# Attention, MoE and gated MoE on one core: the attention's engines each a step apart

## The chip, the cores and the metric

One core of a Trainium2 chip runs one program. The metric is the device time of one execution in microseconds: 684.07 us is the median of three runs of the kernel before (683.9 to 685.65). Five engines work in queues of their own, each in the order in which its instructions were written: TensorE (PE, matrix products and transposes, results to PSUM), VectorE (DVE), ScalarE (ACT), GpSimd (POOL, which here works on SBUF only) and SyncE (SP, which starts the transfers). PSUM has eight banks, here of 512 numbers in each of 128 partitions.

## The reference

Causal attention over 2 batches, 12 heads, 448 positions and head size 64; its result, 896 tokens of 768 numbers, goes through a first MoE layer (one expert) and a second, gated one.

```python
scores = scale * q @ k.T;  scores = where(mask, -1e9, scores)
attn = exp(scores - max(scores));  attn = attn / (sum(attn) + 1e-9)
x = (attn @ v)                                   # to (896, 768)
h = x @ w_in;  g = where(h >= 1, h, where(h <= -1, 0, (h + 1)**2 / 4));  x = g @ w_out
xn = x / sqrt(mean(x*x) + 1e-6) * rms_g
out = (silu(xn @ w_gate) * (xn @ w_val)) @ w_out2
```

## The kernel before

**Products in pairs.** The weights arrive as 64-bit numbers. A *weight step* is a quarter of the work on one block of 128 x 768: scaling of a half on GpSimd (L146), the sign (L151), the high bits (L157) and the low bits (L163) on VectorE, and then the split into a rounded part and a rest on GpSimd (L172, L178). Each block of a layer is then multiplied in three products (L344, 128x448 each), rounded by rounded, rounded by rest, rest by rounded.

**Attention in units.** Two heads are done at a time, in halves of the partitions; such a pair is a *group*, six groups to a batch, twelve in all. A group has three *units*, n = 3g, 3g+1, 3g+2, by rows of the score matrix cut in blocks of 112: the last block row (448 columns for each head), the third and the first (336 and 112), the second (224). For a unit:
- `scores(n)`: on TensorE, for each of the two heads a product of an identity with the mask (L249) that opens the score bank, and the products of q and k (L254). Units take two of four banks in turn (0 to 3), so `scores(n)` waits until the exponentials of unit n-2 have read these banks;
- `maxima(n, j)`: VectorE's negative row maxima of head j (L260);
- `exps(n, j)`: ScalarE's exponentials with their sums (L268), to SBUF;
- `transposes(n)`: on TensorE, the blocks of the exponentials turned over (L284), into banks of a second ring, two for the first two units and one for the third;
- `evac(n, i)`: the copy of the i-th of these banks to SBUF, on ScalarE (L301) or VectorE (L303).

For a group there are besides: `factor` (reciprocals of the sums on VectorE, L309 and L310, and their broadcast on GpSimd, L311), `spread` (that broadcast turned over on TensorE, L317, and copied by ScalarE, L318), `pv` (the P·V products into bank 7, L329), `xsplit` (P·V times the reciprocals on VectorE, L335, and the two parts of X on GpSimd, L336 and L337), the scaling of q two groups ahead (`scale_q`, L228) and the loads.

**The second ring** has banks 4, 5 and 6, and one of them also serves `spread`. In the second batch bank 6 leaves it: columns 0 to 7 of the first MoE layer (first half of the tokens, whose X is then ready) are filled in between, in *parts* of three products (`push_in`, `pump`), six parts to a column, all in bank 6. When a column's six parts are done, `moe_act` works on it (ScalarE L352 and L353, VectorE L354), and only then may the next column begin in the bank. `fillin` takes as many parts as an even share of its calls asks for; what is left is done behind the loop by `pump(len(fill))`.

**What sets the order.** The order of each queue is written out by hand: the loop over n calls these functions, and each engine does its part in the order of the calls. `w_pace` calls weight steps, 0.15 blocks per turn of the loop in the first batch and 0.55 in the second, up to 13 blocks. Turn n of the loop before: scores of n+2; at the head of a group spread and P·V of the group before; transposes of n; then in turn maxima and exponentials of head 0 of n+1, the first copy of n, maxima and exponentials of head 1 of n+1, the second copy of n.

**Behind the attention** the MoE layers run as one dense stream of products on TensorE, with the weight steps beside it.

## Time and profile before

| | |
|---|---|
| median of three runs | 684.07 us |
| profiled execution, its time | 680.13 us |
| its span | 678.4 us |
| mean granted TensorE clock | 0.964 |
| PE / DVE / ACT / POOL busy | 625.6 / 417.5 / 226.1 / 259.9 us |
| DMA, mean | 96 GB/s, 65.03 MB |

The durations are those of one profiled execution; times in it count from the start of its span. A busy time is a mean over stages with different limits: the attention fills about the first 198 us, where TensorE has gaps, and the MoE layers the rest, where it has nearly none. A row that ends in "[1.11 <-ACT af L268]" says that the engine had been idle 1.11 us before it and that the end of ScalarE's line 268 released it. PEclk is the granted clock as a share of 2.4 GHz; at 0.5 it is 1.2 GHz.

### The profile page before, as it was taken

The numbers are of one execution on the slowest core, as the hardware profiler recorded it, in microseconds if no ns is written. First come the engines' busy times: TensorE is split into PE (matmuls) and PEld (weight loads), VectorE is DVE, ScalarE is ACT, GpSimd is POOL, SyncE is SP. The second block draws the span as 40 slices with busy tenths as digits, with TensorE's granted clock in tenths as the row PEclk, the third lists the DMA queues.
The fourth block names the chain that finished last, engine by engine and source line by source line (L and its number), as shares of the span: only waits on it lengthen the run. The fifth ranks groups of instructions, "written<-read, shape, count | busy, mean of one in ns | idle before, by whom it ended". The sixth has DMA issues, their size and how long they took to land.

```text
span 678.4 us, 8418 instructions
## 1 busy us (share of the span) xinstructions
PE 625.6 (92%) x3244; PEld 536.2 (79%) x3244; DVE 417.5 (62%) x547; ACT 226.1 (33%) x492; POOL 259.9 (38%) x207
## 2 busy tenths in 40 slices
PE   6777768977799999999999989999999999999997
PEld 3444435655589999989989978999999999999997
DVE  3435554644548577785153687998988877798300
ACT  3454444544434444422152225112122221332100
POOL 2332475644564645462000152244443344336200
PEclk9788989977899999999999998999999999999999
DMA  6123142313122444342000141223233243336101
GB/s 228 49 90 119 42 135 87 134 61 107 48 94 95 145 137 151 128 146 84 1 0 1 47 140 47 93 94 130 103 112 122 93 127 107 93 121 187 68 29 41
DMA packets 16696, 65.03 MB, mean 96 GB/s; under 512 B 2000, under 2 KB 6608, under 8 KB 16656
## 3 DMA queue, kind: packets, MB, share of 16 engines
q1 hardware_dynamic: 16656, 64.50, 28.9%
q8 instruction: 25, 0.41, 0.3%
q14 instruction: 15, 0.12, 0.1%
HBM read 61.74 MB, written 2.75 MB: 95 GB/s over the span
## 4 chain that ended last, share of the span: by engine, by line
PE 83%; DVE 7%; ACT 7%; issue 2%; DMA 0%; ACTq 0%; SPq 0%
PE b L344 42%; PE b L543 14%; PE b L653 13%; PE b L329 5%; PE b L254 4%; ACT af L268 4%; PE b L284 2%; DVE af L157 2%; DVE af L163 1%; ACT af L301 1%; DVE ar L498 1%; PE b L317 1%; PE b L249 1%; DVE nm L260 1%; DVE af L354 1%
## 5 line engine op out<-in xcount | busy, mean ns | idle before, releaser
L344 PE MATMUL b<-ar 128*128 128x448 f32 x1440 | 303.8, 370 | 11.8 <-DVE af L354 11.8
L344 PEld LDWEIGHTS b<-ar 128*128 128x128 f32 x1440 | 270.1, 189 | 39.6 <-DVE af L354 13.8
L178 POOL TENSOR_TENSOR ar<-af,ar 128x768 fp32r<-128x768 f32 x68 | 128.9, 1896 | 193.4 <-ACT ar L170 192.3
L543 PE MATMUL b<-ar 128*128 128x448 f32 x576 | 121.2, 371 | 3.8 <-DVE ar L498 3.4
L543 PEld LDWEIGHTS b<-ar 128*128 128x128 f32 x576 | 109.0, 190 | 15.6 <-DVE ar L498 4.6
L146 POOL TENSOR_SCALAR af<-af 128x768 f32<-128x768 f32 x68 | 73.2, 1077 | 93.4 <-DMA af<-in_w_out 44.4
L170 ACT CAST ar<-af 128x768 fp32r<-128x768 f32 x55 | 45.9, 835 | 174.0 <-DVE af L163 168.8
L163 DVE SCALAR_TENSOR_TENSOR af<-af 128x768 int32<-128x768 int32 x68 | 87.7, 1290 | 1.8
L653 PE MATMUL b<-ar 128*128 128x448 f32 x432 | 87.7, 365 | 0.0
L653 PEld LDWEIGHTS b<-ar 128*128 128x128 f32 x432 | 81.1, 188 | 6.4
L157 DVE SCALAR_TENSOR_TENSOR af<-af 128x768 int32<-128x768 int32 x68 | 78.4, 1153 | 1.8
L151 DVE TENSOR_SCALAR af<-af 128x768 int32<-128x768 int32 x68 | 53.5, 787 | 8.4 <-POOL af L146 8.4
L268 ACT ACTIVATE af<-b,nm 112x336 f32<-112x336 f32 (+2 forms) x96 | 47.4, 499 | 31.5 <-DVE nm L260 31.3
L498 DVE TENSOR_TENSOR ar<-af,ar 128x448 fp32r<-128x448 f32 x32 | 28.5, 893 | 47.7 <-ACT ar L497 47.5
L354 DVE SCALAR_TENSOR_TENSOR af<-af,b 128x448 f32<-128x448 f32 x32 | 19.8, 619 | 40.9 <-ACT af L353 40.8
L249 PE MATMUL b<-maskb,identb 112*112 112x112 bf16 (+1 forms) x72 | 16.0, 238 | 31.1 <-ACT af L268 29.0
L254 PEld LDWEIGHTS b<-af 64*112 64x112 f32 x192 | 16.0, 193 | 36.0 <-issue 27.3
L301 ACT COPY af<-b 112x448 f32<-112x448 f32 x48 | 25.6, 533 | 45.4 <-PE b L284 44.9
L619 DVE TENSOR_TENSOR af<-af 128x448 f32<-128x448 f32 x24 | 35.4, 1476 | 7.3 <-ACT af L617 6.3
L254 PE MATMUL b<-af 64*112 64x448 f32 (+3 forms) x192 | 37.0, 488 | 2.5 <-DVE af L228 2.5
L260 DVE TENSOR_REDUCE nm<-b 112x1 f32<-112x336 f32 (+2 forms) x96 | 36.8, 436 | 3.1 <-PE b L254 3.1
L497 ACT CAST ar<-af 128x448 fp32r<-128x448 f32 x32 | 18.0, 565 | 56.6 <-PE b L543 56.5
(52 smaller groups left out, 408.8 us busy)
## 6 DMA issues: line engine op xcount, KB each, us to landing
af<-in_w_out SPq DMA_DIRECT2D x28, 768.0 KB, 4.3
af<-in_w_in SPq DMA_DIRECT2D x16, 768.0 KB, 4.3
af<-in_w_gate SPq DMA_DIRECT2D x12, 768.0 KB, 4.2
af<-in_w_val SPq DMA_DIRECT2D x12, 768.0 KB, 4.3
af<-in_kT SPq DMA_DIRECT2D x12, 224.0 KB, 3.5
af<-in_qT SPq DMA_DIRECT2D x12, 224.0 KB, 3.8
af<-in_v SPq DMA_DIRECT2D x12, 224.0 KB, 2.7
out_T<-af SPq DMA_DIRECT2D x12, 224.0 KB, 2.0
```

Of the source, the lines that this page charges most:

```text
L146: nc.gpsimd.tensor_scalar(out=c, in0=c, scalar1=2.0 ** -112, scalar2=1.0, op0=ALU.mult, op1=ALU.mult)
L151: nc.vector.tensor_scalar(out=wt[n % 2].bitcast(I32), in0=words(n, 1, I32), scalar1=-2 ** 31, scalar2=0, op0=ALU.bitwise_and, op1=ALU.bitw ...
L157: nc.vector.scalar_tensor_tensor(out=t, in0=words(n, 1, I32), scalar=3, in1=t, op0=ALU.logical_shift_left, op1=ALU.bitwise_or)
L163: nc.vector.scalar_tensor_tensor(out=t, in0=words(n, 0, I32), scalar=29, in1=t, op0=ALU.logical_shift_right, op1=ALU.bitwise_or)
L170: nc.scalar.copy(dst[:, 0, :], wt[n % 2])
L178: nc.gpsimd.tensor_tensor(out=dst[:, 1, :], in0=wt[n % 2], in1=b32(dst[:, 0, :]), op=ALU.subtract)
L254: nc.tensor.matmul(bs[j][:C, o:o + (c + 1) * C], lhsT=q[r, c * C:(c + 1) * C], rhs=k[r, :(c + 1) * C], start=False, stop=True, skip_group_ ...
L260: nc.vector.tensor_reduce(out=stat[g][0][:C, j, c:c + 1], in_=sbank[n][j][:C, o:o + (c + 1) * C], axis=AX.X, op=ALU.max, negate=True)
L268: nc.scalar.activation(Pn[:C, j, poff[c]:poff[c] + w], sbank[n][j][:C, o:o + w], ACTF.Exp, bias=nm[:C, j, c:c + 1], accum_out=sums[:C, j, ...
L344: nc.tensor.matmul(out, lhsT=w[:, a, k * P:(k + 1) * P], rhs=x[:, c, k], start=(k == 0 and n == 0), stop=(k == NK - 1 and n == 2))
L543: nc.tensor.matmul(ybs[dm][:, :S], lhsT=w[:, a, dm * P:(dm + 1) * P], rhs=t[:, c], start=(n == 0 and i == 0), stop=(n == NM - 1 and i == 2))
L653: nc.tensor.matmul(ob[:, :S], lhsT=w2[dm][:, kk // NK, a, kk % NK], rhs=x[:, c], start=(kk == 0 and i == 0), stop=(kk == NF - 1 and i == 2))
```

## The change

The functions stay as they are; the loop calls them in another order; ahead of it only the scores of unit 0 are done. Turn n now has the scores of n+1, maxima and exponentials of n with the copies of n-2 among them, and the transposes of n-1 at its end; spread and P·V stand in the group's second turn, the X split in its third, `factor` in its first. The loop has one turn more. The filling-in starts with turn 24 (before 21) and counts on three calls of `fillin` per turn.

```diff
@@ -434,48 +434,47 @@
             quota -= k
 
     scores(0)
-    maxima(0, 0)
-    exps(0, 0)
-    maxima(0, 1)
-    exps(0, 1)
-    scores(1)
-    last = NN + 2
+    last = NN + 3
     for n in range(last):
         g, u = divmod(n, NU)
-        if n == NP * NU + 3:
+        if n == NP * NU + 6:
             for m in range(NFILL):
                 push_in(m, 0)
             tring.remove(6)
-            left[0] = 2 * (last - n)
-        if n + 2 < NN:
-            scores(n + 2)
-        if u == 0 and g:
-            spread()
-            pv(g - 1)
-            load_v(g + 1)
+            left[0] = 3 * (last - n)
+        if n + 1 < NN:
+            scores(n + 1)
         fillin()
+        side = nc.vector if g < NP else nc.scalar
+        old = 2 <= n < NN + 2
         if n < NN:
-            transposes(n)
-        more = n + 1 < NN
-        if more:
-            maxima(n + 1, 0)
-            exps(n + 1, 0)
+            maxima(n, 0)
+        if old and u == 1:
+            evac(n - 2, 0, nc.scalar)
         if n < NN:
-            evac(n, 0, nc.scalar)
-        if more:
-            maxima(n + 1, 1)
-            exps(n + 1, 1)
-        if n < NN and u < 2:
-            evac(n, 1, nc.vector if g < NP else nc.scalar)
-        if (n + 1) % NU == NU - 1 and more:
-            factor((n + 1) // NU)
+            exps(n, 0)
+        if old and u != 1:
+            evac(n - 2, 0, nc.scalar)
+            evac(n - 2, 1, side)
+        if n < NN:
+            maxima(n, 1)
+            exps(n, 1)
         if u == 0:
             if g:
+                factor(g - 1)
+        elif u == 1:
+            load_qk(g + 3)
+            if g:
+                spread()
+                pv(g - 1)
+                load_v(g + 1)
+                fillin()
+        else:
+            if g:
                 xsplit(g - 1)
-        elif u == 1:
             scale_q(g + 2, nc.gpsimd)
-        else:
-            load_qk(g + 3)
+        if 1 <= n <= NN:
+            transposes(n - 1)
         flush()
         w_pace(RATE[0] if n < NP * NU else RATE[1])
         fillin()
```

ScalarE, third group of the first batch (b_ numbers are PSUM tiles: b_273, b_274 and b_295, b_296 the scores of its second and third unit, b_319 and b_352 transposes of its first and second). Before:

```order
L268 ACTIVATE af,sums<-b_245,nm 112x448
L318 COPY af<-b_301 128x448
L268 ACTIVATE af,sums<-b_273,nm 112x336
L268 ACTIVATE af,sums<-b_273,nm 112x112
L301 COPY af<-b_319 112x4x112
L268 ACTIVATE af,sums<-b_274,nm 112x336
L268 ACTIVATE af,sums<-b_274,nm 112x112
L268 ACTIVATE af,sums<-b_295,nm 112x224
L301 COPY af<-b_352 112x4x112
L268 ACTIVATE af,sums<-b_296,nm 112x224
```

and now (scores b_271, b_272 and b_296, b_297; transposes b_289 of the unit before the group, b_331 of its first):

```order
L301 COPY af<-b_289 112x2x2x112
L268 ACTIVATE af,sums<-b_271,nm 112x336
L268 ACTIVATE af,sums<-b_271,nm 112x112
L268 ACTIVATE af,sums<-b_272,nm 112x336
L268 ACTIVATE af,sums<-b_272,nm 112x112
L318 COPY af<-b_313 128x448
L268 ACTIVATE af,sums<-b_296,nm 112x224
L301 COPY af<-b_331 112x4x112
L268 ACTIVATE af,sums<-b_297,nm 112x224
```

The copy of the first unit's transposes stood between the exponentials of the second unit; now it stands between those of the third.

GpSimd, X split (L336, L337), broadcast of the reciprocals (L311), scaling of q (L228) and weight steps, fourth group. Before:

```order
L336 TENSOR_SCALAR ar<-af 128x448
L337 TENSOR_TENSOR ar<-af,ar 128x448
L311 TENSOR_SCALAR af<-rs 112x512
L228 TENSOR_SCALAR af<-af 128x448
L172 TENSOR_SCALAR ar<-af 128x768
L178 TENSOR_TENSOR ar<-af,ar 128x768
```

and now:

```order
L336 TENSOR_SCALAR ar<-af 128x448
L337 TENSOR_TENSOR ar<-af,ar 128x448
L228 TENSOR_SCALAR af<-af 128x448
L311 TENSOR_SCALAR af<-rs 112x512
L146 TENSOR_SCALAR af<-af 128x768
L336 TENSOR_SCALAR ar<-af 128x448
```

The scaling of q has moved from behind the broadcast to in front of it.

TensorE, the end of the attention (L344 filled-in parts of columns, L284 transposes, L317 and L329 spread and P·V of the last group, then the dense products). Before:

```order
L284 MATMUL b_1415<-ident,af 112x112 x4
L344 MATMUL b_1407<-ar 128x448 x9
L284 MATMUL b_1447<-ident,af 112x112 x4
L344 MATMUL b_1407<-ar 128x448 x3
L317 MATMUL b_1462<-ident,af 128x112 x4
L329 MATMUL b_1468<-af 64x336 x2
L329 MATMUL b_1468<-af 64x112 x2
L329 MATMUL b_1468<-af 64x336 x2
L329 MATMUL b_1468<-af 64x224 x2
L329 MATMUL b_1468<-af 64x112 x2
L344 MATMUL b_1479<-ar 128x448 x18
L344 MATMUL b_1508<-ar 128x448 x18
```

and now:

```order
L284 MATMUL b_1416<-ident,af 112x112 x4
L344 MATMUL b_1406<-ar 128x448 x6
L317 MATMUL b_1432<-ident,af 128x112 x4
L329 MATMUL b_1438<-af 64x336 x2
L329 MATMUL b_1438<-af 64x112 x2
L329 MATMUL b_1438<-af 64x336 x2
L329 MATMUL b_1438<-af 64x224 x2
L329 MATMUL b_1438<-af 64x112 x2
L344 MATMUL b_1406<-ar 128x448 x9
L344 MATMUL b_1464<-ar 128x448 x18
L344 MATMUL b_1486<-ar 128x448 x18
L344 MATMUL b_1508<-ar 128x448 x18
```

Behind the last P·V there stood one column of 18 products and then the second half's columns; now half a column and two columns stand there first.

## Rows read from the trace of the kernel before

**Rows 1.** Stretches: us, busy (count) PE, PEld, DVE, ACT, POOL, clock, DMA, GB/s.
```profile
20.83:84.30 63.47, 47.92 (x332) 29.35 (x331) 30.50 (x72) 30.74 (x100) 24.37 (x26) 0.90 0.25 80
84.30:118.66 34.36, 25.21 (x157) 16.47 (x156) 18.54 (x30) 15.20 (x46) 21.24 (x18) 0.87 0.34 110
118.66:191.84 73.18, 60.51 (x346) 43.68 (x344) 39.27 (x67) 32.49 (x95) 38.83 (x34) 0.86 0.25 83
191.84:198.50 6.66, 5.88 (x40) 4.75 (x40) 4.24 (x4) 1.36 (x3) 5.49 (x5) 1.00 0.45 149
198.50:678.40 479.90, 472.49 (x2309) 434.10 (x2307) 317.19 (x356) 138.01 (x225) 164.72 (x111) 0.99 0.29 94
```

**Rows 2.** Page's costliest groups: busy, mean ns, idle before and its releaser.
```profile
L249 PE MATMUL b<-maskb,identb 112*112 112x112 bf16 (+1 forms) x72 | 16.0, 238 | 31.1 <-ACT af L268 29.0
...
L301 ACT COPY af<-b 112x448 f32<-112x448 f32 x48 | 25.6, 533 | 45.4 <-PE b L284 44.9
```

**Rows 3.** Timeline, third group: start us, us, engine, line, what.
```profile
34.05 2.11 PE L329 MATMUL b<-af 112*64 112x336 f32 x20
...
36.10 0.98 PE L284 MATMUL b<-ident,af 112*112 112x112 f32 x8
...
36.78 0.53 ACT L301 COPY af<-b 112x448 f32<-112x448 f32 x1 [1.17 <-PE b L284]
...
37.11 0.62 DVE L303 COPY af<-b 112x448 f32<-112x448 f32 x1 [3.86 <-PE b L249]
...
38.24 0.21 PE L249 MATMUL b<-maskb,identb 112*112 112x112 bf16 x1 [1.11 <-ACT af L268]
...
38.35 0.56 POOL L336 TENSOR_SCALAR ar<-af 128x448 fp32r<-128x448 f32 x1 [5.87 <-DVE af L335]
...
38.38 1.01 PE L254 MATMUL b<-af 64*112 64x448 f32 x4
...
41.34 1.10 DVE L260 TENSOR_REDUCE nm<-b 112x1 f32<-112x448 f32 x2
...
42.00 0.64 ACT L268 ACTIVATE af<-b,nm 112x448 f32<-112x448 f32 x1 [1.02 <-DVE nm L260]
```

**Rows 4.** Busy time in the group of rows 3.
```profile
34.05:45.30 11.25, 8.41 (x67) 5.33 (x66) 5.79 (x14) 6.21 (x20) 6.60 (x7) 1.00 0.33 117
```

**Rows 5.** Groups by shape, GpSimd, 20.9 to 84.4 us.
```profile
L337 POOL TENSOR_TENSOR ar<-af,ar 128x448 fp32r<-128x448 f32 x5 | 5.7, 1138 | 0.4
L311 POOL TENSOR_SCALAR af<-rs 112x512 f32<-112x512 f32 x5 | 4.4, 889 | 4.1 <-DVE rs L310 4.1
L228 POOL TENSOR_SCALAR af<-af 128x448 f32<-128x448 f32 x5 | 3.8, 761 | 0.0
L336 POOL TENSOR_SCALAR ar<-af 128x448 fp32r<-128x448 f32 x5 | 3.7, 741 | 33.9 <-DVE af L335 33.9
```

**Rows 6.** Groups by shape, VectorE, same stretch.
```profile
L157 DVE SCALAR_TENSOR_TENSOR af<-af 128x768 int32<-128x768 int32 x3 | 2.8, 921 | 0.0
```

**Rows 7.** Timeline, the dense products behind the last P·V.
```profile
194.73 9.59 PE L344 MATMUL b<-ar 128*128 128x448 f32 x46 [0.78 <-DVE af L354]
```

**Rows 8.** Timeline, border between two weight columns.
```profile
112.14 0.86 PE L344 MATMUL b<-ar 128*128 128x448 f32 x3
...
114.99 0.87 PE L344 MATMUL b<-ar 128*128 128x448 f32 x3 [1.99 <-DVE af L354]
```

**Rows 9.** Timeline, GpSimd's first X operation beside a weight step.
```profile
88.10 0.95 DVE L163 SCALAR_TENSOR_TENSOR af<-af 128x768 int32<-128x768 int32 x1
88.27 1.20 POOL L336 TENSOR_SCALAR ar<-af 128x448 fp32r<-128x448 f32 x1 [7.21 <-DVE af L335]
```

**Rows 10.** Timeline, TensorE at a lower granted clock.
```profile
58.87 3.80 PE L329 MATMUL b<-af 112*64 112x336 f32 x20
...
142.08 1.84 PE L254 MATMUL b<-af 64*112 64x448 f32 x4
...
146.25 1.70 PE L284 MATMUL b<-ident,af 112*112 112x112 f32 x8
```

## The prediction

> **What bounds the kernel now.** I read the page's costliest groups first, then the busy time by stretch, then one attention group instruction by instruction. Three things are to be seen.
>
> First, where the loss lies. From the first P·V product (20.83 us) to the twelfth (191.84) TensorE is busy 47.92 of 63.47 us, 25.21 of 34.36 and 60.51 of 73.18, at a mean granted clock of 0.86 to 0.90; behind it, 472.49 of 479.90 at 0.99 [rows 1]. So only the attention has idle time to give, 15.6 + 9.2 + 12.7 = 37.4 us, and a shift of the attention's end is carried to the end of the kernel nearly whole.
>
> Second, who waits. The largest waits there are ScalarE's copies of transposed blocks on TensorE's transposes (44.9 us of the page's 45.4), and TensorE's mask products on ScalarE's exponentials (29.0) [rows 2]. They are one loop. In the group from 34.05 the P·V products take 2.11 us, the transposes start at 36.10, ScalarE's copy can start only at 36.78, and behind that copy in ScalarE's queue stands the second exponential of the unit, whose end lets the mask product start at 38.24 [rows 3]. ScalarE stood idle while TensorE worked on P·V, and TensorE then idles 1.11 us for ScalarE.
>
> Third, what a group costs without that. The best group lasts 11.25 us, with TensorE busy 8.41, ScalarE 6.21, VectorE 5.79 and GpSimd 6.60, all at clock 1.00 [rows 4]. No engine is full, so the order of waits is the bound.
>
> **The change part by part.** TensorE's own order of scores, P·V and transposes does not change in the first batch; the order pieces of the change show ScalarE's copies moved behind the first exponential of one unit later. The counts of exponentials, transposes and P·V products stay; of the copies one goes from VectorE to ScalarE. The wait for the transposes goes to a place where they are long done, except in one step of three (the unit behind P·V).
>
> *One group of the first batch.* Count from the start of the scores of the third unit. TensorE's sum is 8.4 us [rows 4]. What can be later than this?
> (a) The loop over the score banks. From the start of the second unit's transposes: 1.01 us to VectorE's copy (36.10 to 37.11), 0.62 for it, 0.57 for a maximum (half of the two at 41.34), 0.74 for the exponential with its sum (0.64 and its read), some 0.15 of hand-over: 3.1 us until the mask may start [rows 3]. TensorE has in that time the rest of these transposes, one unit's scores, the third unit's transposes and one mask, about 2.5 us. So 0.6 is added: 9.0.
> (b) The loop through GpSimd: spread and P·V 2.6 us; then in VectorE's queue the copy of the next transposes (1.01 + 0.62 after them), a maximum under 0.57 and the product with the reciprocals, as long as the copy, 2.6 together; then GpSimd's two X operations 0.74 + 1.14, now the scaling of q 0.76 too, then the broadcast of the reciprocals 0.89, on which the next spread waits [rows 5]: 8.7. The change moves the scaling of q in front of that broadcast, which before stood behind it. GpSimd's sum in these groups is 24.37 / 5 = 4.9 [rows 1], so weight steps take 1.35 of it; a third of them falls between: 0.45, which makes 9.2.
> (c) VectorE's weight steps, 0.92 us each [rows 6], lie in loop (a) where they fall behind the second unit: 0.15 x 3 = 0.45 of them per group, 0.4 us.
> I take 9.2 + 0.4 = 9.6 a group, as the two loops share TensorE; ends 8.4 (TensorE alone) and 11.25 (today's best). Five groups: 63.5 - 48.0 = **15.5 us gained**, and for the filling of the pipeline up to the first P·V, which now starts at 20.83 [rows 1] after the same kind of waits, one group's **3.1** (ends 0 and 4).
>
> *Two groups at the head of the second batch.* Weight steps come 3.7 times as often there, and the filling-in of MoE products now starts three steps later, so these two groups hold none, where before, by the order, the second held eight parts of three. The three stretches' GpSimd sums say who binds: 21.24 us in the two groups, 10.6 each [rows 1], more than TensorE's 8.4. With some waiting for the weights' transfer I take 11.5 (ends 10.6 and 14). 34.4 - 23.0 = **11.4 gained**.
>
> *Four groups with filling-in.* Thirty parts of three products lie in them by the order, 7.5 a group; a product costs 0.208 us in a dense row (9.59 us for 46) [rows 7], so 4.7 a group, and TensorE needs 13.1. Between two weight columns there is one bank: from the start of a column's last part at 112.14 to the next column's first at 114.99 are 2.85 us, of which 0.62 is the part: 2.2 of wait [rows 8]. Four such borders lie in the stretch. One is worse than before, since its activation stands in ScalarE's queue before the copies on which the next transposes wait (2.9), the others are partly covered by scores or P·V (0.9, 1.35, 1.3): 1.6 a group. With 0.3 for the rest, 15.0 (ends 13.1 and 17). 73.2 - 60.0 = **13.2 gained**.
>
> *The end.* The twelfth P·V is now followed by 15 parts (three of one column, two whole columns) where before 18 products stood there: 2.1 + 15 x 0.62 + 2 x 2.2 = 15.8 against 6.7 (191.84 to 198.5) [rows 1]: **9.1 given back**. The last X split (VectorE and GpSimd, about 3 us) hides behind these parts.
>
> Behind that point nothing moves on any engine; at most 13 weight blocks may be ready by then in both kernels, since no slot is free for more, so no preparation is lost by coming earlier. DMA: the same transfers in less time, at 80 to 110 GB/s against 149 in the busiest stretch shown [rows 1]. SyncE's order changes only within a group.
>
> Sum: -3.1 - 15.5 - 11.4 - 13.2 + 9.1 = -34.1 us. The profiled execution lasted 680.13 us (its span 678.4, and 1.7 around it that does not change), 3.9 under the median of the runs; so 646.0 for it, and against the median, 684.07, **650.0 us**.
>
> **A rule that speaks against the change.** Where VectorE and GpSimd work at once, rows show both stretched: GpSimd's X operation takes 0.56 us at 38.35 and 1.20 at 88.27 beside VectorE's weight step [rows 3, 9]. The Trainium skill, "SBUF — State Buffer", section "SBUF: two separate sides", says that the two engines share a port pair as an exclusive lock and the loser blocks fully. By that rule a denser attention overlaps them more often, which is the first rival below; the trace agrees that both are stretched.
>
> **Rivals.**
> 1. *GpSimd becomes the bound (smaller gain).* With stretched durations, 1.20, 1.7, 0.8 and 1.3, loop (b) is 2.6 + 2.6 + 5.0 + 0.45 = 10.7 a group: five groups lose 5 more; the two groups with dense weight steps go to 14 (5 more); the four to 16 (4 more). 650.0 + 14 = 664. For it: GpSimd's X operation waits for VectorE in nearly every group, so it has slack today only because the group is slow. Against it: in the first batch its mean durations are 0.74 to 1.14, near the short ones [rows 5].
> 2. *The clock stays down (slower).* Rows show P·V at 3.80 us instead of 2.11 where it was granted less, four scores products at 1.84 instead of 1.01, eight transposes at 1.70 instead of 0.98 [rows 3, 10]. A group wholly at 1.2 GHz costs 1.7 us more for P·V, 0.72 x 2.5 = 1.8 for 20 transposes and 0.83 x 2.5 = 2.1 for the scores: 5.6, over eleven groups 62; some 90 products filled in, 0.208 more each at half the clock, 19: 81 us in all. The gain of 34.1 is eaten when four tenths of the attention run at 1.2 GHz, a mean granted clock of 0.79; at 0.70 (six tenths) the time is 684.1 - 34.1 + 49 = 699. For it: the clock is already 0.86 to 0.90 with idle gaps of 1 us at each unit [rows 1, 3]. Against it: the best group, which has the least idle time, was granted 1.00 throughout [rows 4]. The Trainium skill, "TensorE: Matmul & The Clock Gate", section "Part 4: PE-mode transpose", states that transposes do not count as TensorE work for raising the clock; by that rule attention packed tighter with transposes would stay slow, and the time would be this rival's. The group at 1.00 holds 20 transposes and the four of the spread, so the trace speaks against it here.
> 3. *Nothing comes of it.* The four filled groups and the end give all back: at 17 a group and three more borders uncovered (2.2 each) 14.6 of it, and if the first batch stays at its best 11.25 another 8, the two groups at 16 another 9: 682. Each of these would have to come at once.
>
> **How the numbers follow.** Forecast (638 to 660): 0.74. Rival 1 (660 to 670): 0.15. Rival 2: 0.07. Rival 3: 0.04. The range takes 638 (filled groups near TensorE's 13.1, first ones near 9.0) to 668 (most of rival 1). A difference under 0.3%, 2 us, cannot be told from none with these runs. Faster 0.89, within 0.3% 0.04, slower 0.07.
>
> **What would show it.** Right: P·V products some 9.6 us apart in the first five groups, 11 to 12 in the next two, 15 in the last four; the copies' wait for transposes down from 45 us to under 15; the masks' wait for exponentials under 10; the first dense product of the second half's columns near 165 us instead of 198.5; clock above 0.90 up to there. Wrong: groups of 10.7 with the spread waiting for GpSimd's broadcast (rival 1), P·V at 3.8 us in most groups (rival 2), transposes waiting for ScalarE in each step, or idle time behind the attention, while weight blocks are late.

## The result and the profile after

The changed kernel takes 654.88 us, the median of four runs (651.13 to 656.9), against 683.99 us for the kernel before beside it: a ratio of 0.957, 95% interval 0.9519 to 0.962. The forecast was 650.0 us, range 638 to 668. The profiled execution took 656.9 us, its span 655.2, at a mean granted clock of 0.987 (0.964 before).

The five stretches, cut as in [rows 1] (first, sixth, eighth and twelfth P·V, then the first dense product of the second half's columns); columns as there:

```profile
17.98:63.28 45.30, 40.15 (x332) 26.52 (x331) 30.36 (x69) 29.94 (x101) 24.90 (x27) 1.00 0.36 113
63.28:89.92 26.64, 20.09 (x142) 12.97 (x141) 22.50 (x37) 13.96 (x45) 23.27 (x20) 0.94 0.54 180
89.92:151.86 61.94, 52.58 (x333) 38.71 (x332) 38.19 (x63) 31.51 (x94) 41.59 (x35) 0.92 0.32 103
151.86:169.20 17.34, 13.36 (x67) 10.95 (x67) 1.78 (x3) 2.95 (x5) 2.56 (x3) 0.90 0.01 4
169.20:655.20 486.00, 476.77 (x2309) 432.41 (x2307) 308.86 (x356) 138.06 (x225) 162.61 (x108) 1.00 0.28 92
```

Against [rows 1]: start -2.85 us, five groups -18.2, two groups -7.7, four groups -11.2, end +10.7, together -29.3: the second half's columns start at 169.20 instead of 198.50. The dense part behind took 6.1 us more than before (486.00 against 479.90), so the profiled execution gained 23.2.

The 26.5 us gained behind the first P·V have two halves. TensorE's idle time (stretch less busy time) fell from 38.2 to 25.0 us. Its busy time, for the same products, fell from 139.5 to 126.2: the granted clock rose in the three attention stretches from 0.90, 0.87 and 0.86 to 1.00, 0.94 and 0.92, and in the five groups alone the busy time fell from 47.92 to 40.15. No run changed the clock by itself; that it rose because the waits went is not shown.

The waits that [rows 2] showed, here by line between 15 and 170 us (busy, mean ns, then the idle time before the instruction and its releaser):

```profile
L344 PE MATMUL b<-ar 128*128 128x448 f32 x148 | 42.1, 416 | 8.8 <-DVE af L354 8.2 <-ACT af L301 0.6
L284 PE MATMUL b<-ident,af 112*112 112x112 f32 x224 | 28.9, 267 | 3.9 <-ACT af L301 3.9
L301 ACT COPY af<-b 112x448 f32<-112x448 f32 x48 | 24.1, 530 | 13.2 <-PE b L284 13.2
L249 PE MATMUL b<-maskb,identb 112*112 112x112 bf16 (+1 forms) x62 | 10.7, 232 | 4.8 <-ACT af L268 4.5
L317 PE MATMUL b<-ident,af 112*128 112x112 f32 x48 | 7.7, 287 | 7.9 <-POOL af L311 7.7
```

The copies' wait for the transposes fell from 44.9 to 13.2 us and the masks' wait for the exponentials from 29.0 to 4.5 (5.1 in the whole execution, to which the 29.0 belongs). What TensorE waits for now is three things of about equal size: filled-in parts for VectorE's L354 (8.2), the spread for GpSimd's broadcast (7.7), masks and transposes for ScalarE (4.5 and 3.9).

One group of the first batch, 36.49 to 45.57, answers to [rows 3]:

```profile
36.49 0.60 PE L317 MATMUL b<-ident,af 112*128 112x112 f32 x4 [1.21 <-POOL af L311]
37.02 2.11 PE L329 MATMUL b<-af 112*64 112x336 f32 x20
...
39.07 0.98 PE L284 MATMUL b<-ident,af 112*112 112x112 f32 x8
...
39.88 0.26 PE L249 MATMUL b<-maskb,identb 112*112 112x112 bf16 x2
...
41.45 0.95 DVE L163 SCALAR_TENSOR_TENSOR af<-af 128x768 int32<-128x768 int32 x1
41.62 1.20 POOL L336 TENSOR_SCALAR ar<-af 128x448 fp32r<-128x448 f32 x1 [5.18 <-DVE af L335]
...
42.32 0.62 DVE L260 TENSOR_REDUCE nm<-b 112x1 f32<-112x448 f32 x1
...
42.97 0.63 ACT L268 ACTIVATE af<-b,nm 112x448 f32<-112x448 f32 x1 [1.33 <-DVE nm L260]
...
44.01 0.56 POOL L228 TENSOR_SCALAR af<-af 128x448 f32<-128x448 f32 x1
...
44.53 0.62 POOL L311 TENSOR_SCALAR af<-rs 112x512 f32<-112x512 f32 x1
...
44.87 0.21 PE L249 MATMUL b<-maskb,identb 112*112 112x112 bf16 x1 [0.91 <-ACT af L268]
...
45.57 0.60 PE L317 MATMUL b<-ident,af 112*128 112x112 f32 x4
```

Behind P·V the transposes come at 39.07, and the mask at 39.88 follows without the 1.11 us of [rows 3]. One wait of 0.91 us for an exponential is left, at 44.87. It goes back to a weight step: L163 at 41.45 stands in VectorE's queue before the maximum at 42.32, for which ScalarE waits 1.33 us (the run "weight order" below, which takes that step away, has 0.35 us there). The 1.21 us at 36.49 are the only wait of a spread for GpSimd's broadcast in these five groups.

### The profile page after: what moved, and what is told of

Read it like the earlier page. It is cut to its first block, busy times and chain, and to the rows that moved or that the text cites. A ratio compares the mean times of both kernels' runs of the same rounds, so it can differ in the third digit from the quotient of the medians.

```text
span 655.2 us, 8419 instructions
## 1 busy us (share of the span) xinstructions
PE 614.5 (94%) x3244; PEld 528.2 (81%) x3244; DVE 410.1 (63%) x546; ACT 224.9 (34%) x493; POOL 260.6 (40%) x207
## 4 chain that ended last, share of the span: by engine, by line
PE 79%; DVE 9%; POOL 5%; ACT 3%; issue 2%; DMA 2%; SPq 1%; POOLq 0%; ACTq 0%; DVEq 0%
PE b L344 44%; PE b L652 14%; PE b L542 13%; PE b L329 4%; PE b L284 2%; DVE ar L497 2%; DVE af L163 2%; DVE nm L260 1%; PE b L254 1%; POOL ar L178 1%; PE b L317 1%; DMA af<-in_w_in 1%; POOL ar L337 1%; DVE af L157 1%; DVE af L151 1%
## 5 line engine op out<-in xcount | busy, mean ns | idle before, releaser
L344 PE MATMUL b<-ar 128*128 128x448 f32 x1440 | 307.9, 372 | 8.8 <-DVE af L354 8.2
L344 PEld LDWEIGHTS b<-ar 128*128 128x128 f32 x1440 | 270.6, 190 | 39.3 <-DVE af L354 10.4
L178 POOL TENSOR_TENSOR ar<-af,ar 128x768 fp32r<-128x768 f32 x68 | 131.2, 1929 | 209.5 <-ACT ar L170 208.3
L146 POOL TENSOR_SCALAR af<-af 128x768 f32<-128x768 f32 x68 | 72.5, 1067 | 91.9 <-DMA af<-in_w_out 43.3
L163 DVE SCALAR_TENSOR_TENSOR af<-af 128x768 int32<-128x768 int32 x68 | 84.9, 1249 | 1.7
L354 DVE SCALAR_TENSOR_TENSOR af<-af,b 128x448 f32<-128x448 f32 x32 | 19.8, 619 | 66.7 <-ACT af L353 66.6
L151 DVE TENSOR_SCALAR af<-af 128x768 int32<-128x768 int32 x68 | 50.0, 736 | 14.3 <-POOL af L146 14.3
L352 ACT ACTIVATE af<-b,half 128x448 f32<-128x448 f32 x32 | 20.3, 634 | 55.2 <-PE b L344 55.2
L254 PE MATMUL b<-af 64*112 64x448 f32 (+3 forms) x192 | 34.3, 457 | 2.3 <-DVE af L228 2.3
L284 PEld LDWEIGHTS b<-ident,af 112*112 112x112 f32 x240 | 24.0, 135 | 14.5 <-ACT af L301 10.0
L284 PE MATMUL b<-ident,af 112*112 112x112 f32 x240 | 31.0, 267 | 5.0 <-ACT af L301 5.0
L618 DVE TENSOR_TENSOR af<-af 128x448 f32<-128x448 f32 x24 | 28.7, 1194 | 6.5 <-ACT af L616 4.5
```

What stands on the lines that cost most here:

```text
L146: nc.gpsimd.tensor_scalar(out=c, in0=c, scalar1=2.0 ** -112, scalar2=1.0, op0=ALU.mult, op1=ALU.mult)
L151: nc.vector.tensor_scalar(out=wt[n % 2].bitcast(I32), in0=words(n, 1, I32), scalar1=-2 ** 31, scalar2=0, op0=ALU.bitwise_and, op1=ALU.bitw ...
L163: nc.vector.scalar_tensor_tensor(out=t, in0=words(n, 0, I32), scalar=29, in1=t, op0=ALU.logical_shift_right, op1=ALU.bitwise_or)
L178: nc.gpsimd.tensor_tensor(out=dst[:, 1, :], in0=wt[n % 2], in1=b32(dst[:, 0, :]), op=ALU.subtract)
L284: nc.tensor.transpose(bs[j][:C, o:o + C], Pn[:C, j, poff[c] + kc * C:poff[c] + (kc + 1) * C], ident[:C, :C])
L344: nc.tensor.matmul(out, lhsT=w[:, a, k * P:(k + 1) * P], rhs=x[:, c, k], start=(k == 0 and n == 0), stop=(k == NK - 1 and n == 2))
```

## The experiments

All runs, cut at the spread products (L317) and at the activation of column 7 (L352), in us; "behind" is the rest of the span. The column "TensorE idle" gives its idle time in the four stretches in front of column 7's activation (to 6th / to 8th / to 12th / to column 7). Ratios are to the kernel before, timed beside each run; that kernel's median beside the runs lay between 678.77 and 683.99 us, so runs are compared by ratio.

| run | first spread | to 6th | to 8th | to 12th | to column 7 | column 7 at | behind | TensorE idle | ratio, 95% |
|---|---|---|---|---|---|---|---|---|---|
| before | 19.90 | 63.46 | 34.84 | 73.17 | 7.31 | 198.68 | 479.7 | 15.6 / 9.2 / 12.7 / 0.8 | 1 |
| after | 17.44 | 45.30 | 26.65 | 61.77 | 18.23 | 169.39 | 485.8 | 5.2 / 6.6 / 9.4 / 4.0 | 0.957 (0.9519-0.962) |
| after again | 18.34 | 45.31 | 26.69 | 58.80 | 18.05 | 167.19 | 479.9 | 5.2 / 6.5 / 9.4 / 4.0 | 0.9614 (0.9574-0.9654) |
| copies later | 16.61 | 49.17 | 34.93 | 72.91 | 7.91 | 181.53 | 484.4 | 7.0 / 9.2 / 13.5 / 1.4 | 0.9811 (0.9758-0.9865) |
| X split later | 21.09 | 69.23 | 35.32 | 74.92 | 6.52 | 207.08 | 479.6 | 18.3 / 8.7 / 15.4 / 0.0 | 1.0096 (1.006-1.0133) |
| both | 16.91 | 49.55 | 31.95 | 74.32 | 6.65 | 179.38 | 484.3 | 6.5 / 8.7 / 14.6 / 0.1 | 0.9714 (0.9669-0.9759) |
| both, spread late | 16.81 | 48.38 | 33.20 | 69.41 | 6.64 | 174.44 | 479.9 | 6.5 / 7.7 / 13.3 / 0.0 | 0.9687 (0.9644-0.9729) |
| broadcast first | 20.14 | 45.95 | 25.51 | 56.68 | 18.01 | 166.29 | 479.4 | 3.8 / 5.8 / 8.8 / 4.0 | 0.9528 (0.9484-0.9571) |
| weight order | 18.26 | 42.49 | 28.49 | 61.85 | 18.03 | 169.12 | 481.9 | 2.7 / 7.6 / 9.4 / 4.0 | 0.9545 (0.9504-0.9586) |
| weight load | 17.79 | 45.30 | 20.69 | 61.64 | 18.07 | 163.49 | 481.4 | 5.1 / 1.3 / 10.1 / 4.0 | 0.9541 (0.95-0.9581) |
| fill at 21 | 17.85 | 45.30 | 30.27 | 58.44 | 17.48 | 169.34 | 481.2 | 5.2 / 5.7 / 10.0 / 4.0 | 0.9664 (0.9621-0.9708) |
| tail banks | 20.05 | 49.20 | 27.36 | 60.48 | 15.75 | 172.84 | 483.3 | 5.2 / 5.8 / 9.4 / 2.0 | 0.9632 (0.9585-0.9679) |
| tail fresh | 18.08 | 46.95 | 27.36 | 60.47 | 11.94 | 164.80 | 484.5 | 5.2 / 5.8 / 9.4 / 0.0 | 0.9476 (0.9426-0.9527) |
| combined | 17.52 | 42.19 | 18.01 | 59.22 | 11.95 | 148.89 | 480.4 | 2.4 / 0.3 / 9.5 / 0.0 | 0.9265 (0.9217-0.9313) |

The changed kernel was run once more to see how far a profile repeats:

> The changed kernel once more, unaltered, as the yardstick for the runs beside it. Both theories: a ratio to the kernel before of 0.957 (0.952 to 0.962), about 655 us; first dense column of the second half at about 169 us in its profile.

Measured 652.79 us. Its first seven groups agree with the first run's to 0.1 us, the four groups differ by 3.0, and the stretch behind the attention takes 479.9 us, as in the kernel before [rows 1], where the first profile had 486.0. The first batch is the same code in "after", "after again", "weight load", "fill at 21" and both tail runs; it takes 45.30 or 45.31 us in four of them, 46.95 and 49.20 in the tail runs. TensorE's idle time there is 5.14 to 5.17 us in all six; what differs is its busy time (44.03 us at a granted clock of 0.92 in "tail banks", 40.15 at 1.00). So the length of a stretch moves by up to 4 us with the clock, and effects are read from the idle time, or from differences above that. What makes the 6 us in the dense part is not known: TensorE is busy in nearly all of it in both, and in the first profile it did 118 products in most stretches of 24 us behind 409 us, against 120 in the repeat, both granted 1.00.

**Which part of the change does it?** Three runs start from the kernel before and add one part each. First the copies alone, a unit later:

```diff
@@ turn n of the loop before @@
         if u == 0 and g:
+            evac(n - 1, 0, nc.scalar)
             spread()
...
-        if n < NN:
-            transposes(n)
...
-        if n < NN:
-            evac(n, 0, nc.scalar)
+        if u and n <= NN:
+            evac(n - 1, 0, nc.scalar)
+            evac(n - 1, 1, nc.vector if g < NP else nc.scalar)
...
-        if n < NN and u < 2:
-            evac(n, 1, nc.vector if g < NP else nc.scalar)
+        if n < NN:
+            transposes(n)
```

> The kernel before with only the copies of the transposes moved behind the exponentials of one unit later; reciprocals, X split, scaling of q and start of the filling-in stay where they were. Theory (ScalarE's wait for transposes is the loss): it gives most of the gain, 18 to 26 us, about 662 us, with groups of the first batch 9 to 10 us long and P.V at 2.1 us. Rival (VectorE's two waits, for the sums and for P.V, are as much of it): 5 to 12 us, about 675.

Measured 668.35 us, a ratio of 0.9811, some 13 us less than before: between the two forecasts, just above the rival's. The five groups fall from 63.46 to 49.17 us, 14.3 of the 18.2 that the whole change gains there, and their idle time from 15.6 to 7.0 (after: 5.2); the second batch gains nothing (34.93 + 72.91). Where its waits went (15 to 180 us: what waits, for what, us in all, times, longest):

```profile
ACT af L268 <- DVE nm L260: 39.2, 22, 4.6
DVE af L335 <- PE b L329: 37.1, 11, 5.1
```

VectorE's wait for P·V (last row) was 20.4 us in the kernel before; of the 37.1 here, 22.5 lie in the second batch. One such place in the timeline, in the first batch:

```profile
49.19 0.62 DVE L335 TENSOR_TENSOR af<-b,af 128x448 f32<-128x448 f32 x1 [3.95 <-PE b L329]
49.73 0.38 DVE L260 TENSOR_REDUCE nm<-b 112x1 f32<-112x224 f32 x1
```

VectorE's product with the reciprocals still stands in the turn of P·V: it waits 3.95 us for P·V, with the next maxima behind it. The other part alone, product and split a turn later, and `factor` too:

```diff
-        if (n + 1) % NU == NU - 1 and more:
-            factor((n + 1) // NU)
-        if u == 0:
+        if u == 1:
             if g:
                 xsplit(g - 1)
-        elif u == 1:
             scale_q(g + 2, nc.gpsimd)
-        else:
+        elif u == 2 and n < NN:
+            factor(g)
             load_qk(g + 3)
```

> The kernel before with only the reciprocals and the X split one turn later; the copies stay. Theory: under 4 us of gain, 680 to 684, since ScalarE's copies still wait for the transposes behind P.V; VectorE's waits for the sums and for P.V go away all the same. Rival: 8 to 15 us, about 672.

Measured 688.26 us, 1% slower than before, which neither forecast had: the broadcast comes a turn later, and TensorE's spread now waits 8.1 us for it (before: not at all), while ScalarE's copies still wait 51.9 us for the transposes (15 to 205 us). Both edits together:

> The kernel before with the copies moved one unit later and with reciprocals and X split one turn later, but the filling-in still from turn 21 and VectorE's and GpSimd's other work as before. Theory (in the second batch the copies help only when VectorE no longer waits for P.V with maxima queued behind it): the second batch falls from 107.9 us in the kernel with copies alone to 90 to 95, the whole within 4 us of the changed kernel, 652 to 660. Rival (the later start of the filling-in and its third place in a turn make the second batch's gain): second batch over 100 us, about 667.

Measured 660.78 us. The second batch takes 106.3 us, so the forecast of 90 to 95 failed and the rival's condition (over 100) holds. VectorE's wait for P·V is down to 7.6 us from 37.1, but most of the second batch's gain is still missing. A row says where it stuck:

```profile
53.91 0.61 POOL L311 TENSOR_SCALAR af<-rs 112x512 f32<-112x512 f32 x1
...
54.58 1.01 PE L317 MATMUL b<-ident,af 112*128 112x112 f32 x4 [2.74 <-POOL af L311]
...
55.68 0.53 ACT L318 COPY af<-b 128x448 f32<-128x448 f32 x1 [4.25 <-PE b L317]
56.10 0.55 ACT L268 ACTIVATE af<-b,nm 112x336 f32<-112x336 f32 x1
```

ScalarE's copy of the spread stands in front of the exponentials, and waits 4.25 us through TensorE for GpSimd. The change had moved that copy behind the second unit's exponentials (it is in the order piece for ScalarE), and the prediction gave that no term. So a last run moves it too:

```diff
@@ the run with both, turn n @@
-            spread()
-            pv(g - 1)
-            load_v(g + 1)
-        fillin()
+        else:
+            fillin()
...
             exps(n + 1, 1)
+        if u == 0 and g:
+            spread()
+            pv(g - 1)
+            load_v(g + 1)
+            fillin()
```

> The kernel before with the copies a unit later and the product with q split off a unit later (as in the run that did both), and besides with the spread, the P.V and what is emitted with them put behind the next unit's exponentials, so that ScalarE's copy of the spread (L318) stands behind those exponentials in its queue; the order of TensorE's own instructions stays. Theory (that copy, in front of the exponentials, makes ScalarE wait for GpSimd's broadcast, and this third moved piece is what was still missing): the five groups of the first batch take 45 to 46 us instead of the 49.5 of the run without it, the second batch with its end 105 to 108 us instead of 112.9, ratio to before 0.952 to 0.962. Rival (what is missing is the load of the weight steps and the emission order on VectorE, not this copy): the first batch stays at 49 us or more, the second batch with its end at 112 or more, ratio 0.968 or more.

Measured 657.92 us, a ratio of 0.9687, just on the rival's side; the stretches lie between the two. The wait itself goes, as the theory said: ScalarE's copies wait 5.8 us for the spread instead of 23.8. But the five groups gain only 1.2 us of the expected 4, and none of it is idle time, which is 6.53 us in both runs: TensorE's busy time fell from 43.02 to 41.85 at a clock of 0.96 instead of 0.93. The second batch with its end takes 109.3 instead of 112.9 (after 106.7, again 103.5), with 2.3 us less idle time. So the copy's place is not shown to matter in the first batch, and gives at most some 2 us in the second. Part of what is left is seen in one place:

```profile
50.79 0.83 POOL L172 TENSOR_SCALAR ar<-af 128x768 fp32r<-128x768 f32 x1
...
51.70 2.13 POOL L178 TENSOR_TENSOR ar<-af,ar 128x768 fp32r<-128x768 f32 x1
...
53.80 0.61 POOL L311 TENSOR_SCALAR af<-rs 112x512 f32<-112x512 f32 x1
...
54.47 0.60 PE L317 MATMUL b<-ident,af 112*128 112x112 f32 x4 [2.74 <-POOL af L311]
55.01 3.35 PE L329 MATMUL b<-af 112*64 112x336 f32 x20
```

GpSimd's two operations of one weight step, 2.96 us, stand before the broadcast; the spread waits 2.74, as in the run before this one, and P·V behind it takes 3.35 us instead of 2.11 (this group was granted 0.84). In the changed kernel, where the steps fall one turn otherwise, the same two operations stand behind the broadcast (L172 at 45.11, behind L311 at 44.53). Not tried by themselves: the phase of the weight steps in this kernel, and the third call of `fillin` in a turn, which the rival of the run with both named. Of the second batch's gain of 8.7 us (115.3 to 106.7 with its end) only 2.7 are idle time (22.6 to 19.9); the rest is busy time at a higher clock, so no single moved piece accounts for it.

**The loop through GpSimd.** The prediction's term (b) has the scaling of q (L228) in front of the broadcast. Changed back:

```diff
         if u == 0:
             if g:
                 factor(g - 1)
+                scale_q(g + 1, nc.gpsimd)
...
-            scale_q(g + 2, nc.gpsimd)
```

> The changed kernel with the scaling of q put back behind the broadcast of the reciprocals on GpSimd. Theory of the prediction (a loop through GpSimd of 9.2 us sets the group of the first batch): each of the five groups 0.3 to 0.7 us shorter and the waits of the spread for the broadcast (10.4 us in all) 3 us less: 652 to 653. Rival (the score bank loop sets it, the spread's waits belong to weight steps): within 1 us of 655.

Measured 647.97 us, a larger gain than either forecast had, though the first batch as a whole is not shorter (45.95 us). The spread's waits for the broadcast fall from 10.4 to 6.4 us, as the theory said, but not group by group. The wait of 1.21 us shown above at 36.49 is gone, and the group that it ended takes 8.68 us instead of 9.96; the next three take 9.09, 8.28 and 8.57 against 9.08, 8.39 and 8.78. So the loop through GpSimd set one of these groups and not the others. The first group takes 11.33 us instead of 9.08. That is not the edit: the run "tail banks", whose code is that of the changed kernel up to its end, shows the same, and both were granted 0.79 in it (first row this run, second row "tail banks"; us, busy PE, PEld, DVE, ACT, POOL, granted clock, DMA, GB/s):

```profile
20.14:31.47 11.33, 10.33 (x69) 6.41 (x67) 5.74 (x14) 5.70 (x20) 3.44 (x4) 0.79 0.40 119
```

```profile
20.05:31.38 11.33, 10.33 (x69) 6.43 (x67) 5.74 (x14) 5.69 (x20) 3.87 (x5) 0.79 0.39 123
```

The five groups' idle time falls from 5.15 to 3.77 us, 0.28 a group.

**Weight steps: their place or their number?** In the first run they leave the group's third turn, with the same number in all; in the second the slow rate of the first batch holds for two groups more, and the lost blocks come later:

```diff
@@ weight order @@
-        w_pace(RATE[0] if n < NP * NU else RATE[1])
+        if u < 2:
+            w_pace(1.5 * (RATE[0] if n < NP * NU else RATE[1]))
@@ weight load @@
-        w_pace(RATE[0] if n < NP * NU else RATE[1])
+        w_pace(RATE[0] if n < NP * NU + 6 else 0.65)
```

> The changed kernel with no weight steps in a group's third turn and 1.5 times as many in the other two, so that none stands on GpSimd between the X split and the broadcast. Order theory: the spread's waits for the broadcast (10.4 us) mostly go, 4 to 7 us less, about 650. Load theory (VectorE and GpSimd are full in the two groups at the head of the second batch, 12.8 and 12.4 of 14.2 us): within 1.5 us of 655, the two groups still 26 us.

> The changed kernel with the slow rate of weight steps (0.15) kept for the two groups at the head of the second batch and 0.65 instead of 0.55 behind them. Load theory: the two groups fall from 26.6 to about 19 us, the four filled ones rise by 1 to 3: 4 to 6 us less, about 650. Order theory: groups shorter by the spread's waits alone, 4.6 us there, and as much again given back behind: 653 to 656.

Measured 649.34 and 649.78 us; the ratios, 0.9545 and 0.9541, overlap in their intervals with those of the changed kernel, so the stretches have to decide. In the first batch the place does: 42.49 instead of 45.30 us, 0.56 a group, at 1.00 in both; TensorE's masks wait 2.05 us for exponentials instead of 3.58, its spreads 0.43 for the broadcast instead of 1.21. In the two groups the number does: another place gives 28.49 us with 7.6 idle, fewer steps 20.69 with 1.3, instead of 26.65 with 6.6. Neither theory holds in both places, and the spread's waits only fell from 10.4 to 7.7 us in the first run. The two groups with fewer steps:

```profile
63.09:83.78 20.69, 19.39 (x141) 13.08 (x142) 12.68 (x28) 13.76 (x45) 12.59 (x13) 0.92 0.40 125
```

TensorE is busy 19.39 of 20.69 us, and VectorE and GpSimd, which had 22.50 and 23.27 of 26.64, only 12.7 and 12.6.

**Start of the filling-in and the tail.** The filling-in from turn 21 again:

```diff
-        if n == NP * NU + 6:
+        if n == NP * NU + 3:
```

> The changed kernel with the filling-in from turn 21 as before, not 24. Theory: TensorE idles 6.5 of 26.6 us in the two groups without it, so the parts drawn forward (about eight) cost 2 us there and save 5 at the end, and a border less stands at the end: 3 to 5 us less, about 651. Rival (each part drawn forward brings its border's wait along, and ScalarE's activations stand in front of the copies): within 1 us of 655.

Measured 657.18 us, the rival's case; column 7 comes at 169.34 as with turn 24. Parts shift between the stretches (30.27 + 58.44 + 17.48 against 26.65 + 61.77 + 18.23), and nothing is gained or lost; the idle time in the four stretches is 24.81 us in all against 25.05. For the tail, first other banks behind the loop, then fresh banks one turn earlier, so that no column there waits for the one before it:

```diff
@@ tail banks @@
+    hbanks = deque([0, 1, 2, 3])
     pump(len(fill))
@@ tail fresh @@
+        if n == last - 1:
+            hbanks = deque([1, 2, 3])
```

> The changed kernel with the two columns left at the end of the attention in the score banks, which are free by then, instead of both in one bank. Theory (each border of two columns in one bank costs TensorE 2 us): two waits go, 4.0 us, and up to 1.6 more if TensorE's lower clock there comes from them: about 650. Rival (the last X split or the weights are late behind them): within 1 us of the changed kernel.

> The changed kernel with the two last columns in banks 1 and 2, which no later product of the next dozen needs at once, instead of bank 0, where the wait came back in front of the second half. Theory: both 2 us waits go, so the eighth activation comes 4 to 5.5 us sooner behind the last P.V (13.8 instead of 18.2 us), about 650. Rival (the matrix products behind it wait for X instead): a wait for GpSimd or VectorE of 2 us or more in front of the second half, no gain.

Measured 654.05 and 645.08 us, where both theories had about 650. The first only moved one of the two waits: column 6 had already got bank 6, and column 7 and the first column behind it shared bank 0. TensorE behind the last P·V, in the first:

```profile
159.61 2.09 PE L344 MATMUL b<-ar 128*128 128x448 f32 x9
163.68 9.12 PE L344 MATMUL b<-ar 128*128 128x448 f32 x36 [1.99 <-DVE af L354]
174.79 2.49 PE L344 MATMUL b<-ar 128*128 128x448 f32 x6 [1.99 <-DVE af L354]
```

and in the second:

```profile
153.34 2.11 PE L329 MATMUL b<-af 112*64 112x336 f32 x20
155.38 11.82 PE L344 MATMUL b<-ar 128*128 128x448 f32 x57
```

There the end takes 11.94 instead of 18.2 us, without idle time.

**All that helped.** Broadcast first, fresh banks, weight steps out of the third turn in the first batch (from turn 3), fewer in the next two groups:

```diff
+        if n == last - 1:
+            hbanks = deque([1, 2, 3])
...
                 factor(g - 1)
+                scale_q(g + 1, nc.gpsimd)
...
-            scale_q(g + 2, nc.gpsimd)
...
-        w_pace(RATE[0] if n < NP * NU else RATE[1])
+        if n >= NP * NU + 6:
+            w_pace(0.65)
+        elif u < 2 and n > 2:
+            w_pace(1.5 * RATE[0])
```

> Four edits to the changed kernel at once: the two last columns each in a bank of its own (1 and 2), the scaling of q behind the broadcast, weight steps at the slow rate up to turn 23 (none in the first three turns nor in a group's third), 0.65 behind. Theory (each removes a wait of its own): attention's end 168 us in the changed kernel, less 1.5 at the start, 2.8 in the first batch, 5.9 in the two groups, 4 to 5 at the end, about 154: a ratio of 0.935 to 0.945, about 640 us. Rival (the waits stand in for one another): no better than the best single edit, 0.953.

Measured 630.72 us, ratio 0.9265: it beats both kernels, and the forecast of 640 too. Its first two stretches, cut at the spreads:

```profile
17.52:59.71 42.19, 39.77 (x332) 26.48 (x331) 31.42 (x71) 30.35 (x102) 22.47 (x26) 1.00 0.38 120
59.71:77.72 18.01, 17.68 (x143) 12.31 (x142) 12.74 (x25) 13.29 (x44) 11.42 (x13) 1.00 0.42 122
```

TensorE is busy 39.77 of 42.19 and 17.68 of 18.01 us, at 1.00: these stretches are bound by TensorE now. Of the 12.2 us of idle time that are left up to column 7, 9.5 lie in the four filled groups, which no edit here was aimed at.

## Why the prediction was right, point by point

**What bounds the kernel: right.** The gain lies in the attention, and in the repeat its shift is carried on whole: 479.9 us behind it, as before [rows 1]. In the first batch the loop of ScalarE's copies and TensorE's masks was the cause: moving the copies alone takes away 8.5 of the 10.4 us of idle time. One thing has no term of its own: the sums start from products at the full clock (8.4 us a group, 0.208 a product), so the clock's half of the gain, 13.3 of 26.5 us, is in them without being named. That it came was a condition, which only rival 2 discusses.

**One group of the first batch: right in kind, 0.5 us too large, because (c) was added to the wrong loop.** Predicted 9.6, measured 45.30 / 5 = 9.06: TensorE busy 8.03, the masks' waits for exponentials 0.72, the one spread's wait 0.24. So loop (a) sets these groups, and its 9.0 was right. Loop (b) without weight steps was right in size too (8.7 in the sum; in the group shown 8.66, from the spread at 36.49 to the end of the broadcast at 45.15), but it ends 0.4 us before TensorE wants the broadcast. TensorE waited for it only in the one group where a weight operation (L146, 0.88 us at 34.17) also stands in front of the broadcast. The prediction added (c), which lies in loop (a), on top of loop (b). The sizes: (c) was 0.4, and the weight order run takes 0.31 a group off the masks' waits; the scaling of q in (b) was 0.76, and putting it back takes away 0.28 a group of idle time. Not foreseen: ScalarE's copy of the spread, whose wait fell from 17.7 to 4.6 us; in the spread-late run, where that wait falls from 23.8 to 5.8, the first batch's idle time stays the same.

**Start: the number is near, in part by luck.** -3.1 predicted, -2.85 measured by the first P·V; the repeat has -1.96 (18.87). Up to the first spread TensorE's idle time fell by only 0.8 us (7.2 to 6.4), its busy time by 1.65 (12.70 to 11.05), at a clock of 1.00 instead of 0.96: no group's worth of waits went.

**Two groups at the head of the second batch: too good by 3.6 us** (23.0 against 26.64). Two steps failed. "These two groups hold none" of the filled-in parts was a miscount: the second holds nine products, 2.59 us together, three parts; the prediction's 30 and 15 parts leave three of the 48 out. And the first group takes 14.23 us, a little over the upper end of 14, because there VectorE is full as well as GpSimd:

```profile
63.28:77.51 14.23, 8.92 (x67) 5.55 (x67) 12.79 (x22) 8.46 (x30) 12.41 (x12) 0.96 0.68 225
```

Its timeline shows the price:

```profile
71.11 1.53 POOL L172 TENSOR_SCALAR ar<-af 128x768 fp32r<-128x768 f32 x1
...
71.98 1.46 DVE L163 SCALAR_TENSOR_TENSOR af<-af 128x768 int32<-128x768 int32 x1
72.72 2.38 POOL L178 TENSOR_TENSOR ar<-af,ar 128x768 fp32r<-128x768 f32 x1
...
75.08 0.87 POOL L146 TENSOR_SCALAR af<-af 128x768 f32<-128x768 f32 x1
...
75.90 0.61 POOL L311 TENSOR_SCALAR af<-rs 112x512 f32<-112x512 f32 x1
...
76.57 1.01 PE L317 MATMUL b<-ident,af 112*128 112x112 f32 x4 [4.00 <-POOL af L311]
```

Three of GpSimd's weight operations pass before the broadcast and the spread waits 4.00 us. That is rival 1 in one group; three other spreads of the eleven wait 0.64 to 1.82 us. The weight-load run takes the two groups to 20.69 us.

The operations are stretched beside each other: L172 takes 1.53 us here and 0.83 in the row at 50.79 above, VectorE's L163 1.46 here and 0.95 at 41.45. In the rows that the prediction gave for this [rows 3, 9], only GpSimd's operation is stretched; the 0.95 us of L163 beside it is no longer than its usual short duration (0.91 to 0.95 us). The Trainium skill, "SBUF — State Buffer", section "SBUF: two separate sides", says that GpSimd and certain VectorE operations, among them those with two SBUF inputs, take the shared port pair as an exclusive lock; the trace agrees that operations of both engines are longer at 71 to 75 us, and no run here shows who held what.

**Four groups: right within the scatter.** 15.0 predicted, 61.94 / 4 = 15.5 measured; 14.7 in the repeat, where the last two of them were granted 1.00 instead of 0.89 and the idle time is the same. The borders were 2.9, 0.9, 1.35 and 1.3; the rows give 3.28, 0.95, 1.32 and 1.99, 0.3 us a group more.

**The end: mechanism right, 1.6 us more than the 9.1 given back.** Both borders cost 1.99 us (2.2 predicted). The 0.62 us of a part was too small, since the clock fell:

```profile
153.90 2.09 PE L344 MATMUL b<-ar 128*128 128x448 f32 x9
157.98 5.47 PE L344 MATMUL b<-ar 128*128 128x448 f32 x18 [1.99 <-DVE af L354]
165.44 6.75 PE L344 MATMUL b<-ar 128*128 128x448 f32 x32 [1.99 <-DVE af L354]
```

18 products take 5.47 us, 0.304 each, against 0.208 in [rows 7].

**The sum.** -34.1 predicted, -29.3 measured up to the dense part: the five groups gained 2.7 us more than forecast; the start gained 0.25, the two groups 3.7 and the four groups 2.0 less, and the end gave back 1.6 more. So part of the errors cancelled. The profiled execution has 6.1 us more in the dense part, which its repeat has not.

**The rivals.** Rival 1: in one group fully, as said. Rival 2, the clock: not to the 0.79 that it needed over the whole attention. The stretches were granted 0.90 to 1.00, the five groups 1.00, and P·V took 2.11 us there; single groups of the same code did fall to 0.79 in other runs (the rows above). The Trainium skill, "TensorE: Matmul & The Clock Gate", "Part 4: PE-mode transpose", says that the full clock does not engage for TensorE's transpose mode; five groups at 1.00 with 24 transposes each show that they did not hold the clock down here, among other products, and the profile does not tell whether they run in that mode. Rival 3: no attention group gave its gain back, and the end gave back 10.7 where 9.1 was reckoned with.

## What to carry to other kernels

When two engines each wait for the other and none is full, look for the one instruction that waits at the head of an in-order queue with needed work behind it, and move it a step later on its own engine; then ask for each further instruction that follows the same product (here P·V's product and the copy of the spread) whether it now takes that place: the first move gave three quarters of the gain in one batch and none in the other. Judge each move by the idle time of the engine that you want to fill: the length of a stretch of the same code moved here by up to 4 us with the granted clock. Once the waits are gone, background work has a price by its place and its amount, and a single bank for consecutive columns has a price wherever nothing else can be put between.

## What the runs showed of the hardware

The clock behind short waits, at the end of the attention in the changed kernel (us, busy PE, PEld, DVE, ACT, POOL, granted clock, DMA, GB/s):

```profile
157.98:163.45 5.47, 5.47 (x18) 4.59 (x18) 0.48 (x1) 0.00 (x0) 2.56 (x3) 0.69 0.00 0
165.44:172.00 6.56, 6.56 (x32) 6.09 (x33) 0.62 (x1) 1.22 (x2) 0.00 (x0) 1.00 0.00 0
```

and at the same place in the run "broadcast first":

```profile
154.88:158.79 3.91, 3.91 (x18) 3.30 (x18) 0.48 (x1) 0.00 (x0) 2.56 (x3) 1.00 0.00 0
160.78:170.10 9.32, 9.32 (x38) 8.52 (x39) 0.62 (x1) 1.38 (x3) 0.00 (x0) 0.82 0.01 2
```

TensorE idles 1.99 us before each of these four rows. In the changed kernel the 18 products behind the first wait had a mean clock of 0.69, that is in part 1.2 GHz, 5.47 - 18 x 0.208 = 1.7 us more than at the full clock, and those behind the second 1.00. In the other run it is the other way round: 18 products in 3.91 us behind the first wait, and 0.82 behind the second. The repeat and "fill at 21" are like the changed kernel, "weight order" and "weight load" like the other run. So each of these six runs paid once, and an equal wait does not lower the clock each time; in the run with fresh banks, without the waits, 57 products in a row at this place took 0.207 us each. And in the dense part two profiles of the same kernel took 486.0 and 479.9 us; what makes that difference stays open.
